# The rows of maxima of 27 heads put by ScalarE's DMA queue instead of SyncE's

## The chip, the cores and the metric

The kernel runs on one core of a Trainium2 chip. Times are device microseconds of one execution. The engines are TensorE (PE, with its weight loads as PEld), VectorE (DVE), ScalarE (ACT), GpSimd (POOL) and SyncE (SP). SP computes nothing here: it issues DMAs, one after the other. ACT computes, and can issue DMAs too; an instruction of an engine's queue starts after the ones ahead of it.

## The reference: bucketed attention and a feed-forward block

```python
q_bucket = np.sum(q_bits * powers, axis=-1)      # bits: sign of q @ proj, 6 of them
mask = q_bucket[:, :, :, None] == k_bucket[:, :, None, :]
scores = np.where(mask, scale * np.matmul(q, k.transpose(0, 1, 3, 2)), -1000000000.0)
attn = np.exp(scores - np.max(scores, axis=-1, keepdims=True))
attn = attn / (np.sum(attn, axis=-1, keepdims=True) + 1e-09)
attn_out = np.matmul(attn, v)                    # 4 batches, 8 heads, 768 tokens, 64 wide
# then, over 3072 tokens of width 512:
h = x @ w_in                                     # 512 -> 2048
g = np.where(h >= 1, h, np.where(h <= -1, 0.0, (h + 1) ** 2 / 4))
out = g @ w_out                                  # 2048 -> 512
```

All in float32, from which the kernel's matmuls work with pairs of a high and a low part.

## The kernel before

Attention comes first (to about 441 us), then the feed-forward block. Attention is one list of units: 32 heads (`hd`), in each two halves of 384 queries, in each six blocks of 128 keys, so 12 units per head, `g` from 0 to 383. A unit (`s_unit`, L432) multiplies keys by queries in two matmuls into one PSUM tile `s` (L439 and L440), ACT takes the exponential twice, as a rounded `ph` (L448) and in full (L453), and `lo_unit` subtracts the two to `pl`, on POOL where `pool_lo(g)` says so and on VectorE otherwise (L39, a helper). Four units later `pv_unit` multiplies both with V (L473, L475, L477).

The mask and the row maxima enter S as extra rows of the operand tiles `T1` and `T2`: rows 0 to 7 of `T2[...][:, 0, h]` hold bits of the query's bucket and, in row 7, the negated maximum of each query. That maximum is found one to two heads ahead: PE multiplies once more (`max_mm`, L361, into the single PSUM pair `smax`), VectorE reduces (`nm`, L378), POOL clamps, PE transposes (L416), ACT copies the result to a small tile `te` (L421), and two DMAs leave from `te`: one sets row 7 of `T2` (L423), the other stores flags to DRAM (L425). The first L440 of the head reads row 7 and so waits for the first of these DMAs. `max_put` of a head runs behind the sixth unit of the head before, so six units lie between it and that matmul. Two buffers of `te` take turns.

Each engine runs its instructions in the order in which this list writes them. So on SP, the row's DMA stands behind whatever the units before wrote there: the finished output of the head before (`xd`, L487, and `sd`, L488), staged weights (L108), loads of the next pair's q and k (`raw`, L174), moves between operand tiles (L190), bits (L316). On ACT, what follows the copy to `te` is the sign of the bits (`neg`, L243), the exponentials, in the even heads (head 4 on) the cast of the next pair's V (L323), and the copies of outputs (L483).

In the kernel before, the row's DMA is issued by ACT for heads 3 and 4 and by SP for heads 5 to 31 (heads 0 and 1 set theirs in another way, and head 2 in halves).

Of the kernel before, what the change touches and what calls it, by code (L numbers as in the profile page):

```python
# [11 lines left out]
F32 = mybir.dt.float32  # L12
# [107 lines left out]
NQK, NV, NP_ = 3, 2, 7  # L120
# [9 lines left out]
def attention(ctx, tc, wst, T1, T2, qk, v, pj, cv, x_d, s_d, e_d, tasks, shared):  # L130
    nc = tc.nc
# [286 lines left out]
    def max_put(hd):  # L418
        pr, h = hd // 2, hd % 2
        te = small.tile([2 * NJ, P], F32R, name="te")  # L420
        (nc.vector.tensor_copy if hd == 0 else nc.scalar.copy)(out=te, in_=mx.pop(hd)[0:2 * NJ, 0:P])  # L421
        if pr > 0:
            (nc.sync if hd > 4 else nc.scalar).dma_start(out=T2[pr % NQK][7:8, 0, h, :].bitcast(F32),  # L423
                                                         in_=te[0:NJ, :].bitcast(F32))
        nc.sync.dma_start(out=e_d[hd // H][hd % H:hd % H + 1, :], in_=te[NJ:2 * NJ, :].bitcast(F32))  # L425

# [199 lines left out]
    at(12, move, 1, 2)  # L626
    at(12, max_tr, 0, 0)
    at(12, max_put, 0)
    at(10, load_raw, 2)
    at(13, move, 1, 3)  # L630
# [5 lines left out]
    for t in VB[1:]:  # L636
        at(12, lambda t=t: nc.gpsimd.memset(t[:, :, 1].bitcast(F32), 0.0))
    at(17, max_tr, 1, 1)
    at(17, max_put, 1)
    at(19, half_put, 2, 0, 1)  # L640
    at(24, half_put, 2, 1)
    for h, g in enumerate((20, 2 * NU + 1)):
        at(g, lambda h=h: nc.gpsimd.memset(T2[0][32:33, 0, h].bitcast(F32), 0.0))
    for hd in range(NH):
        pr, h = hd // 2, hd % 2
        g = hd * NU
        if 0 < hd < NH - 2:
            gc, gt = ((30, 32), (41, 43))[hd - 1] if hd < 3 else (g + NU + SHIFT - 1, g + NU + SHIFT + 1)
            at(gc, max_clamp, hd + 2, nc.gpsimd)
            at(gt, max_tr, hd + 2)  # L650
            at(gt, max_put, hd + 2)
# [730 lines left out]
```

## Time and profile before

| | |
|---|---|
| median of 3 runs | 928.15 us (926.03 to 929.7) |
| the profiled execution | 927.39 us, span 925.6 us |
| PE busy | 904.9 us, 98% of the span |
| ACT busy, whole span | 667.1 us, 72% |
| ACT busy, 80 to 427 us (attention with rows put by SP) | 315.65 of 347 us |
| PE idle at L440, ended by `t<-te` | 3.4 us, 6 times |
| PEld idle at L440, ended by `t<-te` | 6.1 us, 9 times |

A row of the timeline has the start in us, the length in us, the engine, the line and the operation, and in square brackets how long the engine was idle before it and what ended that. SPq and ACTq are instructions of the queues that issue DMAs; they do not count as the engine's busy time. A matmul of 384 columns is shown 0.33 us long, but the next one may start 0.16 us after it.

### The profile page before, as it was taken

The page shows a single profiled execution, that of the slowest core. Times are in us where ns is not written, and L with a number is a line of the kernel's source. Part 1 is how long each engine was busy: PE and PEld are TensorE (multiplying, and loading weights), DVE is VectorE, ACT ScalarE, POOL GpSimd, SP SyncE. Part 2 cuts the span into 40 slices and gives each one's busy share as a digit, 9 for nine tenths or more (in the row PEclk, how much of TensorE's full clock was granted, in tenths as well). Part 3 has the DMA queues.
Part 4 walks back from the last instruction along what each step waited for, and adds up shares of the span by engine and source line. Part 5 has one row for each costly group of instructions (what it writes and reads, how often), then busy time and mean ns, then how long its engine had stood idle before and what let it go on. Part 6 is the DMA issues. An engine that isn't in the chain of part 4 may idle for free.

```text
span 925.6 us, 15771 instructions
## 1 busy us (share of the span) xinstructions
PE 904.9 (98%) x5050; PEld 846.4 (91%) x5050; DVE 746.3 (81%) x1319; ACT 667.1 (72%) x1471; POOL 352.3 (38%) x464
## 2 busy tenths in 40 slices
PE   8999999999999999999999999999999999999997
PEld 7789999999998999999999998989999999999996
DVE  8988889888897889887798888878877788765564
ACT  7889998999988999999656566555565555554454
POOL 7877777888787787778100000000000000000000
PEclk9999999999999999999999999999999999999999
DMA  5774676666666676564496388987559564464431
GB/s 159 195 201 109 181 195 194 191 181 180 175 179 187 188 193 184 140 185 123 144 307 228 114 245 299 317 259 204 149 152 271 156 200 127 147 178 126 125 91 68
DMA packets 95689, 167.66 MB, mean 181 GB/s; under 512 B 14532, under 2 KB 52536, under 8 KB 95608
## 3 DMA queue, kind: packets, MB, share of 16 engines
q1 hardware_dynamic: 95344, 166.63, 62.3%
q8 instruction: 40, 0.66, 0.3%
q14 instruction: 41, 0.34, 0.1%
q10 hardware_dynamic: 264, 0.03, 0.0%
HBM read 106.13 MB, written 33.96 MB: 151 GB/s over the span
## 4 chain that ended last, share of the span: by engine, by line
PE 71%; DVE 11%; ACT 7%; DMA 5%; issue 4%; POOL 1%; DVEq 0%; ACTq 0%; SPq 0%; POOLq 0%
PE y L913 24%; PE h L1145 16%; PE h L1050 6%; DMA t<-te 4%; PE s L440 4%; PE smax L361 4%; PE o L477 3%; PE o L473 3%; PE o L475 3%; PE s L439 3%; DVE nm L378 3%; DVE pl L39 3%; PE o L237 2%; ACT ph L448 2%; ACT s L453 1%
## 5 line engine op out<-in xcount | busy, mean ns | idle before, releaser
L448 ACT ACTIVATE ph<-s 128x384 fp32r<-128x384 f32 x380 | 193.0, 508 | 31.3 <-PE s L440 28.5
L39 POOL TENSOR_TENSOR pl<-pf,ph 128x384 fp32r<-128x384 f32 x154 | 156.0, 1019 | 67.9 <-ACT pf L453 67.7
L378 DVE TENSOR_REDUCE nm<-smax 128x1 f32<-128x768 f32 x168 | 160.1, 953 | 22.5 <-PE smax L361 19.4
L39 DVE TENSOR_TENSOR pl<-s,ph 128x384 fp32r<-128x384 f32 x230 | 123.6, 549 | 22.6 <-ACT s L453 18.3
L878 DVE SCALAR_TENSOR_TENSOR t<-t 128x384 f32<-128x384 f32 x128 | 71.3, 557 | 85.9 <-ACT z L873 85.6
L440 PE MATMUL s<-t 128*128 128x384 f32 x384 | 126.2, 329 | 3.5 <-DMA t<-te 3.4
L477 PE MATMUL o<-pl,va 128*128 128x384 f32 x384 | 125.7, 327 | 1.0 <-POOL pl L39 0.6
L473 PE MATMUL o<-ph,va 128*128 128x392 f32 (+1 forms) x384 | 126.0, 328 | 0.6 <-DVE neg L248 0.6
L475 PE MATMUL o<-ph,vb 128*128 128x392 f32 (+1 forms) x384 | 125.8, 328 | 0.0
L439 PE MATMUL s<-t 128*128 128x384 f32 x384 | 125.7, 327 | 0.0
L913 PE MATMUL y<-t,ghi 128*128 128x512 f32 x384 | 118.3, 379 | 0.7 <-DMA wc<-tmp 0.7
L453 ACT ACTIVATE s<-s 128x384 f32<-128x384 f32 x226 | 115.7, 512 | 0.0
L361 PE MATMUL smax<-t 128*128 128x384 f32 x336 | 85.9, 337 | 4.0 <-DVE nm L378 3.3
L883 ACT CAST ghi<-z 128x384 fp32r<-128x384 f32 x129 | 64.9, 503 | 32.0 <-DVE z L879 31.7
L873 ACT ACTIVATE z<-t,m 128x384 f32<-128x384 f32 x128 | 78.8, 615 | 4.2
L440 PEld LDWEIGHTS s<-t 128*128 128x128 f32 x384 | 72.5, 189 | 6.3 <-DMA t<-te 6.1
L913 PEld LDWEIGHTS y<-t,ghi 128*128 128x128 f32 x384 | 71.0, 189 | 7.4 <-ACT ghi L883 1.3
L453 ACT ACTIVATE pf<-s 128x384 f32<-128x384 f32 x154 | 77.5, 503 | 0.0
L1145 PE MATMUL h<-wbig,t 128*128 128x384 f32 x399 | 76.6, 326 | 0.3 <-DVE wsq L1164 0.3
L879 DVE TENSOR_TENSOR z<-t,z 128x384 f32<-128x384 f32 x128 | 71.4, 558 | 4.5
L477 PEld LDWEIGHTS o<-pl,va 128*128 128x128 f32 x384 | 72.6, 189 | 2.4 <-POOL pl L39 1.5
L913 PE MATMUL y<-woh,glo 128*128 128x512 f32 x192 | 73.1, 381 | 0.8 <-DVE glo L887 0.8
(208 smaller groups left out, 2003.3 us busy)
## 6 DMA issues: line engine op xcount, KB each, us to landing
t<-wc SPq DMA_DIRECT2D x92, 256.0 KB
t<-t SPq DMA_DIRECT2D x60, 384.0 KB
wraw<-wc SPq DMA_DIRECT2D x76, 256.0 KB
raw<-in_qk_dram SPq DMA_DIRECT2D x14, 768.0 KB
wraw<-in_w_in_dram SPq DMA_DIRECT2D x16, 512.0 KB
wraw<-in_w_out_dram SPq DMA_DIRECT2D x16, 512.0 KB
t<-ed SPq DMA_DIRECT2D x36, 192.0 KB
xd<-xs SPq DMA_DIRECT2D x32, 192.5 KB
```

Of the source, the lines that this page charges most:

```text
L39: eng.tensor_tensor(out=out, in0=a, in1=b, op=ALU.subtract)
L361: nc.tensor.matmul(out=into(ps[:, 0:HS]), lhsT=t2[:, 0, h, i * P:(i + 1) * P], rhs=streamed(t2[:, 1, h, hf * HS:(hf + 1) * HS]), start=Tru ...
L378: nc.vector.tensor_reduce(out=nmp(hd)[:, i:i + 1], in_=smax[hd][:, :, 0:HS], axis=AX.XY, op=ALU.max, negate=True)
L439: nc.tensor.matmul(out=into(ps[:, 0:HS]), lhsT=t1[:, 1, h, ks], rhs=streamed(t1[:, 0, h, sl]), start=True, stop=False)
L440: nc.tensor.matmul(out=into(ps[:, 0:HS]), lhsT=t2[:, 1, h, ks], rhs=streamed(t2[:, 0, h, sl]), start=False, stop=True)
L448: nc.scalar.activation(out=ph[:, 0:HS], in_=ps[:, 0:HS], func=AF.Exp, scale=SCALE)
L453: nc.scalar.activation(out=pf, in_=ps[:, 0:HS], func=AF.Exp, scale=SCALE)
L473: nc.tensor.matmul(out=into(o[:, 0:w]), lhsT=wa, rhs=streamed(ph[:, 0:w]), start=(jj == 0), stop=False)
L475: nc.tensor.matmul(out=into(o[:, 0:w]), lhsT=wb, rhs=streamed(ph[:, 0:w]), start=False, stop=False)
L477: nc.tensor.matmul(out=into(o[:, 0:HS]), lhsT=wa, rhs=streamed(pl), start=False, stop=(jj == NJ - 1))
L913: nc.tensor.matmul(out=into(ys[c][m]), lhsT=g_[:, m * P:(m + 1) * P], rhs=streamed(w), start=(first and k == 0), stop=(last and k == 2))
L1145: nc.tensor.matmul(out=into(ps), lhsT=w[:, cs], rhs=streamed(x), start=(n == 0 and s not in (2, 3, 6)), stop=(n == 5), skip_group_check=True)
```

## The change

One expression: the engine that issues the DMA of row 7. What is copied, from where and to where, is the same.

```diff
         if pr > 0:
-            (nc.sync if hd > 4 else nc.scalar).dma_start(out=T2[pr % NQK][7:8, 0, h, :].bitcast(F32),
+            nc.scalar.dma_start(out=T2[pr % NQK][7:8, 0, h, :].bitcast(F32),
                                                          in_=te[0:NJ, :].bitcast(F32))
         nc.sync.dma_start(out=e_d[hd // H][hd % H:hd % H + 1, :], in_=te[NJ:2 * NJ, :].bitcast(F32))
```

On ACT, at the place in head 8 (an even head) where the row of head 9 is put; `va` is the cast of V, `neg` the sign of the bits. Before:

```order
L421 CAST te<-s 12x128
L243 ACTIVATE neg<-o_142 32x384
L448 ACTIVATE ph_163<-s 128x384
L453 ACTIVATE pf<-s 128x384
L323 CAST va_156<-vraw 128x6x2x64
L448 ACTIVATE ph_164<-s 128x384
L453 ACTIVATE s<-s 128x384
```

And now, as far as it differs:

```order
L421 CAST te<-s 12x128
L423 DMA t_1_82<-te 1x6x128
L243 ACTIVATE neg<-o_142 32x384
L448 ACTIVATE ph_163<-s 128x384
L453 ACTIVATE pf<-s 128x384
```

The DMA stands directly behind the copy that feeds it, and ahead of `neg`; the rest of ACT's order is the same.

On SP, the place in an odd head where the row of the next even head (head 8, whose operand tile is `t_1_82`) was put; `wq` is a staged weight, `em` the store of the flags:

```order
 L488 DMA sd_63<-xs 1x768
 L108 DMA wq_98<-wsq 128x512
-L423 DMA t_1_82<-te 1x6x128
 L425 DMA em_72<-te 6x128
 L190 DMA t_2_80<-t_2_83 64x1536
```

SP no longer issues the row; the output, the weight and the flags keep their places. The same happens at each of the 27 heads. The orders on PE, VectorE and POOL do not change.

## The prediction

> **What bounds the kernel now.** I read the page first, then the waits of the attention stretch, then single stretches of the timeline. The page:
>
> ```profile
> PE 904.9 (98%) x5050; PEld 846.4 (91%) x5050; DVE 746.3 (81%) x1319; ACT 667.1 (72%) x1471; POOL 352.3 (38%) x464
> PE y L913 24%; PE h L1145 16%; PE h L1050 6%; DMA t<-te 4%; PE s L440 4%; PE smax L361 4%; PE o L477 3%; PE o L473 3%; PE o L475 3%; PE s L439 3%; DVE nm L378 3%; DVE pl L39 3%; PE o L237 2%; ACT ph L448 2%; ACT s L453 1%
> ```
>
> PE bounds the kernel as a whole, but the page's averages mix two stages, and the change lies in attention only. The 4% for `t<-te` in the chain (37 us) is not what the transfer costs: the chain follows it from issue to landing, while PE works on other things for most of that time. The stretch where the rows move, and the same stretch's waits, say more (columns of the first row: length, then busy us and count of PE, PEld, DVE, ACT, POOL; of the others: us in total, times, longest):
>
> ```profile
> 80.00:427.00 347.00, 338.79 (x2014) 324.16 (x2014) 302.56 (x454) 315.65 (x773) 275.18 (x348) 1.00 0.64 177
> ACT ph L448 <- PE s L440: 24.2, 61, 0.7
> DVE pl L39 <- ACT s L453: 14.4, 22, 1.0
> PEld smax L361 <- DVE nm L378: 10.7, 25, 0.6
> PEld s L440 <- DMA t<-te: 6.1, 9, 1.2
> PE s L440 <- DMA t<-te: 3.4, 6, 0.9
> ```
>
> ACT is busy 315.65 of 347 us (91%) here, not 72%, and 24.2 of its 31 idle us are waits for PE: a cover, but a broken one. PE's largest wait is for VectorE's maxima (`nm`); the rows of maxima come second. VectorE itself waits for ACT's exponentials 22 times, so an ACT delay can reach PE by way of VectorE.
>
> **What the change moves.** 27 issues, heads 5 to 31, go from SP's queue to ACT's; heads 3 and 4 are there already and give the price:
>
> ```profile
> L423 SPq DMA_DIRECT2D t<-te x27: 755/765/785, 81.8 to 425.3; - x27
> 57.45 0.25 ACT L421 CAST te<-s 12x128 fp32r<-12x128 f32 x1
> 57.73 0.73 ACTq L423 DMA_DIRECT2D t<-te  x1
> 58.51 0.48 ACT L243 ACTIVATE neg<-o 32x384 f32<-32x384 f32 x1 [0.81 <-PE o L477]
> 70.50 0.68 ACTq L423 DMA_DIRECT2D t<-te  x1
> 71.22 0.49 ACT L448 ACTIVATE ph<-s 128x384 fp32r<-128x384 f32 x1 [0.75 <-PE o L477]
> 73.99 0.33 PE L439 MATMUL s<-t 128*128 128x384 f32 x1
> 74.15 0.33 PE L440 MATMUL s<-t 128*128 128x384 f32 x1
> ```
>
> The label blames PE, but the idle time is exactly the issue: ACT does nothing for 0.81 and 0.75 us while its queue issues. So 27 puts put 27 x 0.78 = 21 us on ACT. On the whole stretch that nearly fits into the 31 idle us; the question is where.
>
> The Trainium skill (DMA: Bandwidth & Descriptors, section "Issuing engines are not separate DMA queues") holds that issuing from another engine saves only the issue time on the sequencer, which it calls usually small. By its 50 ns for sequencer dispatch (same page, "Anatomy of one DMA — SWDGE (gpsimd) path") I estimate 27 x 0.05 = 1.4 us on ACT and the change would be a small gain; the rows above show fourteen times that, and they decide.
>
> **The gain.** A put on SP is late and lands late (the chain's rows are start, us; a wait's length stands in square brackets):
>
> ```profile
> 200.25 0.25 ACT L421 CAST te<-s 12x128 fp32r<-12x128 f32 x1
> 199.20 1.91 SPq L487 DMA_DIRECT2D xd<-xs  x1
> 202.13 0.76 SPq L423 DMA_DIRECT2D t<-te  x1
> 202.13 4.83 DMA t<-te
> 206.36 0.33 PE L439 MATMUL s<-t 128*128 128x384 f32 x1
> 207.00 0.43 PE L440 MATMUL s<-t 128*128 128x384 f32 x1 [0.31 <-DMA t<-te]
> ```
>
> The row of head 14 is ready at 200.50, SP issues it 1.63 us later because xd and what follows it stand ahead, and it lands 4.83 us after issue. PE's two S matmuls start 0.64 us apart where 0.16 is normal (73.99 and 74.15 above): 0.48 lost. PE's idle of 3.4 us hides 0.17 at each of its 6 places (0.33 long at a pace of 0.16), so about 4.4, and with the three short ones that only the weight load shows some 4.9 us are lost in all. On ACT's queue the issue comes right behind the copy, and row 4 was there by 74.15, at most 3.65 us after its issue. A row issued at 200.53 would then land by 204.2, 2.3 us ahead of need. I take all nine stalls as gone. What is late next is VectorE's maximum:
>
> ```profile
> 208.44 0.95 DVE L378 TENSOR_REDUCE nm<-smax 128x1 f32<-128x768 f32 x1
> 209.73 0.49 PE L361 MATMUL smax<-t 128*128 128x384 f32 x2
> 182.04 0.96 DVE L378 TENSOR_REDUCE nm<-smax 128x1 f32<-128x768 f32 x1 [0.20 <-PE smax L361]
> 183.48 0.49 PE L361 MATMUL smax<-t 128*128 128x384 f32 x2
> ```
>
> At head 14 VectorE works without idle into the reduction that ends at 209.39; PE's next maximum at 209.73 needs it and can come 0.3 earlier, not 0.48. At head 12 (0.91 lost, the label says 0.75 idle) the reduction can start 0.2 earlier, which lets the maximum at 183.48 come 0.6 earlier. So some 60% of 4.9 is kept, 2.9 us; from this goes what ACT's own delay has left on VectorE there (next part).
>
> **The cost.** Two kinds of places. First the even heads, where the rows of the odd heads 5 to 27 are put (12 puts):
>
> ```profile
> 187.08 0.25 ACT L421 CAST te<-s 12x128 fp32r<-12x128 f32 x1
> 187.59 0.48 ACT L243 ACTIVATE neg<-o 32x384 f32<-32x384 f32 x1 [0.26 <-PE o L237]
> 188.85 0.83 ACT L323 CAST va<-vraw 128x768 fp32r<-128x768 f32 x1
> 189.96 0.50 ACT L453 ACTIVATE s<-s 128x384 f32<-128x384 f32 x1
> 197.50 0.49 ACT L448 ACTIVATE ph<-s 128x384 fp32r<-128x384 f32 x1 [0.69 <-PE s L440]
> 190.55 0.56 DVE L39 TENSOR_TENSOR pl<-s,ph 128x384 fp32r<-128x384 f32 x1 [0.86 <-ACT s L453]
> 191.02 0.95 DVE L378 TENSOR_REDUCE nm<-smax 128x1 f32<-128x768 f32 x1
> 192.11 0.34 PE L361 MATMUL smax<-t 128*128 128x384 f32 x1
> 196.49 0.59 PE L361 MATMUL smax<-t 128*128 128x384 f32 x2 [0.22 <-DVE nm L378]
> ```
>
> The put goes between 187.33 and 187.59; 0.81 of idle replaces 0.26, so `neg` and all behind it slide 0.55 us. ACT has no further idle time until 197.50: the cast of V (0.83) stands behind it. The exponential that ends at 190.46 ends at 191.01, and VectorE, which already waits 0.86 us for it, starts its subtraction 0.55 later. The reduction behind it ends at 192.52 instead of 191.97, and PE's maximum matmul at 192.11 must wait for it, some 0.45 us; at 196.49, where PE waits for VectorE already, the full 0.55 has arrived. PE has no slack to win it back: its matmuls follow each other at 0.16 us. So 12 x 0.55 = 6.6 us. At heads 5 and 7 there is no 0.26 to use (the next row), so 0.79 each: together 7.1 us.
>
> ```profile
> 81.84 0.48 ACT L243 ACTIVATE neg<-o 32x384 f32<-32x384 f32 x1
> 204.11 0.49 ACT L448 ACTIVATE ph<-s 128x384 fp32r<-128x384 f32 x1 [0.20 <-PE s L440]
> 208.67 0.49 ACT L448 ACTIVATE ph<-s 128x384 fp32r<-128x384 f32 x1 [0.33 <-PE s L440]
> ```
>
> Second, the odd heads, where the rows of 6 to 28 are put (12 puts; 200.25 is one). No cast of V follows, ACT's slide of about 0.6 is cut by waits for PE at 204.11 (0.20) and 208.67 (0.33), and VectorE does not wait for ACT at a point where PE waits for VectorE. I cost these at nothing, hidden under those waits, except that about 0.3 is still on VectorE around 207 and eats the gain there: of 2.9 us I keep 1.5. Without that cover they would cost as the first kind, another 12 x 0.55 = 6.6.
>
> Third, rows 29 to 31, put where no `neg` follows:
>
> ```profile
> 424.40 0.25 ACT L421 CAST te<-s 12x128 fp32r<-12x128 f32 x1 [0.27 <-PE s L416]
> 424.83 0.49 ACT L448 ACTIVATE ph<-s 128x384 fp32r<-128x384 f32 x1 [0.18 <-PE s L440]
> ```
>
> Head 31's comes 15 us before the end of attention, with ACT at work almost throughout: 0.81 less 0.18 is a slide of 0.6. PE uses an exponential four units later, so between 0 and 0.6 shows; I take 0.5 for all three. SP loses 27 x 0.765 = 21 us of issues; PE waits for no transfer of SP's but these rows there, so I price that at nothing (bounds 0 to 1 us gain).
>
> Sum: 7.1 + 0.5 - 1.5 = +6.1 us. The profiled execution took 927.39 us, 0.76 under the median of the three runs (928.15). 927.39 + 6.1 = 933.5, which I forecast; it would be 934.3 on the median.
>
> **Rivals.** (1) The cover holds on even heads too: place, the maximum at 192.11; if that slide costs PE a third (0.2 us of 0.55, because VectorE catches up in the 0.5 us it idles later in the head), the cost is 2.5 + 0.5, and the gain kept is between 2.9 and 4.9: 927.4 + 3 - 3.9 = 926.5, not slower. It decides from a slide under about 0.25 us per head. For it: the 24.2 us that ACT waits for PE. Against it: none of them lies between 187.6 and 197.5. (2) The issue is dearer on ACT while SP issues its large loads: SP's own xd took 1.91 us at 199.20 behind a load, against 0.77 for SP's puts. If ACT's put is held the same way at the 12 odd heads (1.1 more each, of which the waits of 0.20 and 0.33 hide 0.5), that is 12 x 0.6 = 7 more: 940.5. Against it: 0.73 and 0.68 are steady, if only twice seen. (3) The move does not do what it says: the rows still queue behind SP's traffic and land as late as now, the stalls stay and the delay is paid, 927.4 + 7.6 = 935. Here the skill's rule that all issuers share the same 16 DMA engines and interleave would speak for it; row 4's 3.65 us against 4.83 for head 14's bears that out only weakly. (4) Both effects are hidden, 927 to 928.5.
>
> **How the numbers follow.** Forecast 0.58, its own range 930 to 937; rival 1 0.15, 2 0.14, 3 0.08, 4 0.05. A change of under 0.5% (4.6 us) cannot be told from none by a measurement of this kernel, so slower means above 932.8. From the forecast 0.36 lies above and 0.22 below; rivals 2 and 3 are slower (0.22); rival 1 gives 0.05 faster and 0.10 the same; rival 4 the same. Slower 0.58, same 0.37, faster 0.05. The low end is 927.4 + 3.5 (half of the even heads' cost) - 3.9 = 927; the high end reaches to rival 2: 940.
>
> **What would show it.** The waits for `t<-te` at L440 vanish (else rival 3). ACT's queue shows 29 puts of about 0.7 us, each with some 0.8 us idle behind (over 1.2 in odd heads: rival 2). At the copy behind each V cast, VectorE's wait for ACT grows from 0.86 to 1.4, and PE's waits for `nm` grow from 10.7 us to about 17; if they stay, rival 1 is right. FFN, 445 us on, keeps its length. The forecast is wrong if attention ends earlier than before.

## The result: slower, 934.91 us

The changed kernel took 934.91 us (median of 6 runs, 933.43 to 935.61), the kernel before 927.43 us on the same chip; the ratio is 1.0077, 95% interval 1.0063 to 1.0091. The forecast was 933.5 us, range 927 to 940. The page of the profile after, whose execution took 934.82 us:

```profile
span 933.0 us, 15779 instructions
PE 909.0 (97%) x5050; PEld 844.9 (91%) x5050; DVE 743.4 (80%) x1319; ACT 663.9 (71%) x1471; POOL 352.0 (38%) x464
```

The first and last matmul `y` of the feed-forward block, of the kernel before and then of the changed one (the last two times of a row are the first and the last start):

```profile
L913 PE MATMUL y<-t,ghi x384: 379/379/483, 449.4 to 866.6; 128*128 128x512 f32 x192
```

```profile
L913 PE MATMUL y<-t,ghi x384: 379/379/483, 456.9 to 874.6; 128*128 128x512 f32 x192
```

The block starts 7.5 us later and keeps its length (417.2 and 417.7 us). All of the loss is in attention. The waits of the changed kernel from 80 to 427 us:

```profile
PEld smax L361 <- DVE nm L378: 20.5, 42, 1.4
DVE neg L248 <- ACT neg L243: 17.9, 21, 1.3
PE smax L361 <- DVE nm L378: 7.4, 27, 1.1
PEld s L440 <- DMA t<-te: 2.6, 6, 0.7
PE s L440 <- DMA t<-te: 1.0, 3, 0.5
```

PE's waits for VectorE's maxima about doubled (the weight load's from 10.7 us, the matmul's from 2.9). Its waits for the row fell by more than half (6.1 and 3.4 before), but did not vanish.

To compare kernels I use one count throughout: from the first L440 of head 4 to that of head 31, for each matmul of PE, the time since the start of the one before, less its normal pace (164 ns for 384 columns), where that is over 40 ns, added up by the line of the matmul that came late. It is worked out from the timeline's rows, for one profiled execution of each kernel, so a single wait that falls differently shows in it. "Even" and "odd" are the lengths of heads 4 to 28 and of heads 5 to 27, from first L440 to first L440.

| | even | odd | head 29 | head 30 | late at L361 | at L440 | at L477 |
|---|---|---|---|---|---|---|---|
| before | 167.2 | 163.8 | 13.03 | 11.31 | 11.3 | 5.0 | 1.5 |
| after | 176.2 | 161.1 | 13.89 | 11.90 | 21.6 | 2.0 | 2.4 |
| e1, odd heads' rows on ACT | 174.7 | 164.8 | 13.45 | 11.88 | 18.6 | 6.1 | 2.9 |
| e2, even heads' rows on ACT | 169.0 | 161.6 | 13.81 | 11.31 | 14.3 | 1.7 | 2.4 |
| e3, before, cast later | 164.4 | 165.6 | 13.04 | 11.30 | 7.5 | 8.5 | 1.0 |
| e4, after, cast later | 168.8 | 167.5 | 13.89 | 11.90 | 19.8 | 2.9 | 3.1 |
| e5, e1 and cast later | 167.2 | 169.3 | 14.47 | 11.88 | 9.4 | 10.8 | 5.0 |
| e9, rows on POOL | 164.9 | 163.1 | 15.00 | 12.02 | 10.1 | 6.2 | 1.8 |
| e10, even heads' rows on POOL | 165.4 | 164.9 | 14.85 | 11.31 | 10.4 | 8.0 | 1.0 |
| e11, before, raw load later | 180.1 | 158.7 | 13.03 | 11.31 | 14.7 | 0.3 | 6.2 |
| e12, before, raw load in halves | 169.0 | 158.9 | 13.03 | 11.31 | 15.2 | 0.2 | 1.0 |

So of +7.8 us after, the even heads lost 9.1, heads 29 and 30 lost 1.45, and the odd heads won 2.7. A head's row is put in the head before it: the row of head 29 in head 28, which is counted with the even heads, those of 30 and 31 in heads 29 and 30.

The place of the prediction's timeline, head 12, in the changed kernel. First ACT, then VectorE, then PE's maxima:

```profile
189.07 0.25 ACT L421 CAST te<-s 12x128 fp32r<-12x128 f32 x1
189.35 0.69 ACTq L423 DMA_DIRECT2D t<-te  x1
190.09 0.48 ACT L243 ACTIVATE neg<-o 32x384 f32<-32x384 f32 x1 [0.76 <-PE s L440]
191.35 0.83 ACT L323 CAST va<-vraw 128x768 fp32r<-128x768 f32 x1
...
190.60 0.55 DVE L248 TENSOR_TENSOR neg<-o,neg 32x384 f32<-32x384 f32 x1 [0.82 <-ACT neg L243]
193.05 0.56 DVE L39 TENSOR_TENSOR pl<-s,ph 128x384 fp32r<-128x384 f32 x1 [1.04 <-POOL pl L39]
193.52 0.95 DVE L378 TENSOR_REDUCE nm<-smax 128x1 f32<-128x768 f32 x1
...
194.52 0.59 PE L361 MATMUL smax<-t 128*128 128x384 f32 x2 [0.23 <-DVE nm L378]
198.99 0.59 PE L361 MATMUL smax<-t 128*128 128x384 f32 x2 [0.22 <-DVE nm L378]
```

ACT's idle time before `neg` is 0.76 us instead of 0.26. VectorE waits 0.82 for `neg` and 1.04 for the exponential behind the cast (the label names POOL, whose subtraction had ended at 192.56; the exponential ends at 192.95, and VectorE starts at 193.05). PE now waits for `nm` once more, at 194.52, still within head 12; the wait at 198.99, in head 13, is the one that stood at 196.49 before. The chain that ended last goes through the put itself (ACTq L423 at 189.35).

### The profile page after: what moved, and what is told of

The parts are those of the page before. It is cut to its first block, busy times and chain, and to the rows that moved or that the text cites. A ratio compares the mean times of both kernels' runs of the same rounds, so it can differ in the third digit from the quotient of the medians.

```text
span 933.0 us, 15779 instructions
## 1 busy us (share of the span) xinstructions
PE 909.0 (97%) x5050; PEld 844.9 (91%) x5050; DVE 743.4 (80%) x1319; ACT 663.9 (71%) x1471; POOL 352.0 (38%) x464
## 4 chain that ended last, share of the span: by engine, by line
PE 63%; DVE 13%; ACT 10%; DMA 5%; issue 5%; POOL 2%; ACTq 1%; DVEq 0%; SPq 0%; POOLq 0%
PE y L913 24%; PE h L1145 16%; PE h L1050 6%; ACT ph L448 4%; DVE nm L378 3%; PE smax L361 3%; DVE pl L39 3%; PE s L440 3%; PE s L439 2%; PE o L477 2%; PE o L473 2%; PE o L475 2%; DMA t<-te 2%; POOL pl L39 2%; ACT pf L453 1%
## 5 line engine op out<-in xcount | busy, mean ns | idle before, releaser
L39 DVE TENSOR_TENSOR pl<-s,ph 128x384 fp32r<-128x384 f32 x230 | 123.6, 549 | 26.2 <-POOL pl L39 12.2
L477 PE MATMUL o<-pl,va 128*128 128x384 f32 x384 | 125.8, 328 | 1.7 <-POOL pl L39 0.9
L440 PE MATMUL s<-t 128*128 128x384 f32 x384 | 125.8, 328 | 1.0 <-DMA t<-te 1.0
L361 PE MATMUL smax<-t 128*128 128x384 f32 x336 | 88.6, 345 | 8.8 <-DVE nm L378 7.8
L361 PEld LDWEIGHTS smax<-t 128*128 128x128 f32 x336 | 54.6, 188 | 24.8 <-DVE nm L378 21.4
L477 PEld LDWEIGHTS o<-pl,va 128*128 128x128 f32 x384 | 72.6, 189 | 3.4 <-POOL pl L39 1.8
L440 PEld LDWEIGHTS s<-t 128*128 128x128 f32 x384 | 72.6, 189 | 2.6 <-DMA t<-te 2.6
## 6 DMA issues: line engine op xcount, KB each, us to landing
xd<-xs SPq DMA_DIRECT2D x32, 192.5 KB
```

The lines of the kernel that those rows point to most:

```text
L39: eng.tensor_tensor(out=out, in0=a, in1=b, op=ALU.subtract)
L361: nc.tensor.matmul(out=into(ps[:, 0:HS]), lhsT=t2[:, 0, h, i * P:(i + 1) * P], rhs=streamed(t2[:, 1, h, hf * HS:(hf + 1) * HS]), start=Tru ...
L440: nc.tensor.matmul(out=into(ps[:, 0:HS]), lhsT=t2[:, 1, h, ks], rhs=streamed(t2[:, 0, h, sl]), start=False, stop=True)
L477: nc.tensor.matmul(out=into(o[:, 0:HS]), lhsT=wa, rhs=streamed(pl), start=False, stop=(jj == NJ - 1))
```

## Which of the puts cost: e1 and e2

e1 puts the odd heads' rows on ACT and leaves the even heads' with SP; e2 does the reverse. Against the kernel before:

```diff
# e1
-            (nc.sync if hd > 4 else nc.scalar).dma_start(
+            (nc.scalar if hd <= 4 or hd % 2 else nc.sync).dma_start(
# e2
+            (nc.scalar if hd <= 4 or hd % 2 == 0 else nc.sync).dma_start(
```

> Only the rows of the odd heads (5 to 31, 14 puts, all but the last two made in even heads) go to ACT's queue; the even rows stay with SP. Theory (ACT's slide reaches PE through VectorE in the even heads, and nowhere else before the last heads): the even heads 4 to 28 grow by 0.5 to 0.8 us each as in the changed kernel, 9 us in all, the stalls at L440 stay (4.9 us lost), so 8 to 10 us over the kernel before, 935.5 to 937.5: dearer than the whole change. Rival (each put costs the same wherever it stands, 7.5 / 27 = 0.28 us): 14 x 0.28 = 3.9, 931.3.

e1: 936.91 us, ratio 1.0092 (1.0073 to 1.0111), as the theory had it.

> Only the rows of the even heads (6 to 30, 13 puts, made in odd heads) go to ACT's queue. Theory: no cost in the even heads beyond 0.1 us, the stalls at L440 shrink from 4.9 to under 2 us, head 30's put costs up to 0.6: 1.5 to 2.5 us under the kernel before, 925 to 926. With the odd rows' run the two differences add up to the change's 7.5. Rival (each put 0.28): 13 x 0.28 = 3.6 more, 931.

e2: 928.58 us, ratio 0.9999 (0.9986 to 1.0012). Neither expectation held. The waits of e1 and then of e2, 80 to 427 us, with two rows of e2's timeline:

```profile
PEld smax L361 <- DVE nm L378: 17.8, 37, 0.7
PEld s L440 <- DMA t<-te: 7.2, 9, 1.2
PE smax L361 <- DVE nm L378: 6.6, 27, 0.4
```

```profile
PEld smax L361 <- DVE nm L378: 13.5, 29, 1.4
PEld s L440 <- DMA t<-te: 2.3, 6, 0.6
...
183.38 0.50 POOL L179 CAST t<-raw 128x384 fp32r<-128x384 f32 x1 [2.59 <-DMA raw<-in_qk_dram]
186.93 0.43 PE L477 MATMUL o<-pl,va 128*128 128x384 f32 x1 [1.19 <-POOL pl L39]
```

e1 carries the whole cost: with its puts alone the even heads grow 7.5 us. e2 has most of the gain at L440 (5.0 to 1.7 us late), wins 2.1 in the odd heads, and loses 0.8 in head 29, where the row of head 30 is put. The 1.8 us that its even heads lose, where it puts nothing, are one wait: head 12 alone grew 2.07, because POOL waited 2.59 us for raw data and PE then for POOL (the two rows; 1.35 us late at L477 and 0.50 at L416); the other twelve even heads are 0.28 shorter together. In the kernel before, such a wait of 2.81 us for raw data stands in head 20.

Of the 3.3 us that the odd heads of e2 win at L440, 1.2 come back at L361 in the same heads, behind the copy to `te`. There L361 is 1.8 us late in the odd heads before, and also in e12 below, where the rows are on time too but SP puts them; it is 3.0 late in e2 and 2.0 in the changed kernel. So the twelve puts in odd heads cost PE 1.2 us in e2 and 0.2 in the changed kernel.

## Does the cast behind the put make it dear: e3, e4, e5

The cast of V is moved nine units on, into the odd head: alone (e3), with the change (e4), and with e1's put (e5).

```diff
-            at(gv, cast_v, pr + 1, nc.scalar)
+            at(gv + (9 if pr > 1 else 0), cast_v, pr + 1, nc.scalar)
```

> The kernel before, with the cast of V moved nine units on (from the unit behind the row's put in each even head from 4 on to the fourth unit of the odd head); rows by SP as before. Theory: VectorE's wait of 0.86 us for ACT behind the cast goes, and with it PE's waits of 0.53 at the maximum in the odd heads 5 to 27: 3 to 6 us under the kernel before, 921 to 924. Rival (VectorE's own weight steps make those waits): no change within 1 us, or up to 3 us slower because the cast now delays the odd heads.

> The same move of the cast of V, in the changed kernel (27 rows by ACT). Theory (the put is exposed because the cast of V stands behind it and ACT has no idle time for 10 us): without the cast, ACT's waits for PE come back in the even heads and hide the put; this kernel stands at most 3 us above the one with the cast moved and rows by SP. Rival (the put's delay reaches PE whatever stands behind it): the distance between the two stays at 6 to 8 us.

> Only the odd heads' rows by ACT (14 puts, made in even heads and before the last two heads), with the cast of V moved out of the even heads. Theory (the cast of V behind the put is what leaves ACT without cover): in the run with all rows by ACT and the cast moved, the even heads from 8 on cost only 0.27 us each over the cast-moved kernel with rows by SP; so 12 x 0.3 to 0.4 and 1.4 for the last rows: 4 to 6 us over that kernel's 926.9, 931 to 933, against 936.9 with the cast in place. Rival (the put costs as much without the cast): 8 to 9.5 over it, 935 to 936.5.

| | median, us | ratio, interval | against e3 |
|---|---|---|---|
| e3 | 926.93 | 0.9985 (0.9973 to 0.9998) | |
| e4 | 932.67 | 1.0046 (1.0029 to 1.0063) | +5.7 |
| e5 | 935.42 | 1.0081 (1.0067 to 1.0095) | +8.5 |

e3's waits, then e5's:

```profile
PEld s L440 <- DMA t<-te: 9.5, 11, 1.8
PEld smax L361 <- DVE nm L378: 7.5, 19, 0.6
PEld o L477 <- POOL pl L39: 0.6, 1, 0.6
```

```profile
PEld s L440 <- DMA t<-te: 12.1, 11, 1.7
PEld smax L361 <- DVE nm L378: 7.7, 17, 0.7
PEld o L477 <- POOL pl L39: 5.5, 12, 2.1
```

The theory lost in all three, in an instructive way; the rival's numbers held in e3 and e5, and e4 fell between the two. e3 took 2.8 us out of the even heads, and the rows came 3.5 us later relative to PE: hardly a gain. e5's puts cost the even heads 2.8 us over e3 instead of 7.5, so the cast behind the put does carry the slide to L361. But the time came out elsewhere: at L477, where PE waits for POOL's subtraction, and at L440, where SP issued the even heads' rows on average 1.16 us behind their copy instead of 0.79, with the copy no later ahead of the matmul (5.61 and 5.52 us). Of the 4.0 us more at L477, 2.0 stand in heads 29 and 30, where POOL also waited 2.70 us for a staged weight (0.86 in e3), so how much of that part the puts cost is open. ACT is busy 91% of the stretch in the kernel before, and what it stands still surfaced in part at whichever wait was next (5.7 us over e3 in e4, which has the early rows too, 8.5 in e5): moving the neighbour decided where more than whether.

## Is it the issue on ACT, or the earlier transfer: e9 and e10

POOL is idle for an exponential of ACT just where the row is put. e9 lets it issue all 27 rows, e10 only the even heads' (13 rows); odd rows stay with SP in e10.

```diff
# e9
-            (nc.sync if hd > 4 else nc.scalar).dma_start(
+            (nc.gpsimd if hd > 4 else nc.scalar).dma_start(
# e10
+            (nc.scalar if hd <= 4 else nc.sync if hd % 2 else nc.gpsimd).dma_start(
```

> The 27 rows are issued by GpSimd (POOL) instead of ScalarE (ACT): as early as in the changed kernel, but on an engine that in the kernel before is busy 275 of 347 us of this stretch and mostly idle 1.0 to 1.75 us for ACT's exponential right where the row is put. Theory (the whole cost of the change is the 0.78 us that ACT stands still per put; an issue on an engine with idle time at that place is free): the cost is gone, 927 us, between 925.5 and 928.5, and the row stalls at L440 stay near the 1.8 us of the changed kernel, since the transfers share the same DMA engines. Rival (the cost comes with the earlier transfer itself, from whichever engine): 933 to 935.5 again. Second rival (an issue holds POOL for over 2 us, so its subtractions come late and PE waits for them at L477): over 936.

> Only the rows of even heads 6 to 30 (14 in all with none of the odd ones) are issued by POOL; those of odd heads stay with SP, which is on time there. Theory: 925 to 927.5, no more than 2.5 us better than before, because the even rows still need 5 to 6 us to land behind the moves. Rival (the earlier transfer costs): 928.5 to 931.

e9: 929.73 us, ratio 1.0012 (0.9999 to 1.0025). e10: 928.73 us, ratio 1.0004 (0.9989 to 1.0018). The waits of e9, one of its puts, three rows of its chain of waits (start, length), and a row of VectorE in head 29:

```profile
POOL t L423 <- ACT te L421: 22.7, 26, 1.2
POOL pl L39 <- ACT pf L453: 15.5, 32, 1.5
PEld smax L361 <- DVE nm L378: 9.8, 16, 2.6
PEld s L440 <- DMA t<-te: 7.5, 11, 2.0
...
200.36 0.61 POOL L423 DMA_DIRECT2D t<-te  x1 [1.19 <-ACT te L421]
...
174.13 6.14 DMA t<-te
200.36 5.95 DMA t<-te
226.42 5.92 DMA t<-te
...
412.34 3.15 DVE L790 SCALAR_TENSOR_TENSOR raw<-t,xsv,raw 128x384 f32<-128x384 f32 x1
```

This separates the two causes. The rows leave nearly as early as in the changed kernel (0.29 us after the copy ends at 200.07, a length of 0.25 after 199.82 in ACT's row; 0.03 there), POOL needs 0.61 us per issue, and PE's waits for `nm` are back at 9.8 us. Of the ratio of 1.0077, 1.0012 is left: the loss was the issue on ACT, not the earlier transfer. The issue is not free on POOL either, but POOL waits less for ACT in return (15.5 us for `pf` and 22.7 for `te`, instead of 56.5 for `pf`). The time missed its range by 1.2 us, on a chip where the kernel before took 928.87. Head 29 takes 2.0 us longer in e9 and 1.8 in e10: there a VectorE instruction between two reductions (L790, the last row above) takes 3.15 and 2.79 us instead of 1.17, and PE's maximum waits 2.28 and 1.82 us for the reduction behind it. Why it is slow when POOL puts the row was not tested.

And neither gains: an even head's row still needs 5 to 6 us from issue to the matmul, from whichever queue. The stalls at L440 are 6.2 us late in e9, not near 1.8 as expected. e10 is 8.0 us late at L440 and loses the 1.8 us in head 29; its expected gain did not come for these two reasons. Its time lies in the rival's range, but e9 speaks against the rival's cause.

## Why the even heads' rows are late: e6, e7, e8, e11, e12

In the changed kernel the row of head 14 stands in the chain of waits as

```profile
202.98 6.57 DMA t<-te
209.59 0.43 PE s L440
```

issued 1.6 us sooner after its copy than before, and still too late by 0.5 us. By the trace's records of single DMA packets, the rows of odd heads 13 to 27 have landed 1.4 to 1.8 us after ACT issues them; those of even heads 12 to 26 begin to move 3.8 to 4.4 us after it and have landed after 5.4 to 6.1. From the issue to the first packet, the DMA engines are busy 0.24 of the time at head 13's row and 0.95 at head 14's (columns as in the prediction's stretch from 80 to 427 us; the last two are the DMA engines' busy share and GB/s):

```profile
189.35:190.77 1.42, 1.42 (x10) 1.42 (x9) 0.60 (x2) 0.66 (x2) 0.00 (x0) 1.00 0.24 60
202.98:207.38 4.40, 4.40 (x29) 4.34 (x28) 3.33 (x7) 3.65 (x9) 2.28 (x4) 1.00 0.95 223
```

What differs is what SP has issued just ahead: three moves of 384 KB and the load of raw q and k, 768 KB. e6 (before), e7 (after) and e8 (e6 with e3's cast) set the three moves behind the row; e11 sets the raw load there instead.

```diff
# e6, e7, e8: moves 0 to 2 of the pair
-                at(g0 + (3 + (pr == 1) if pr < 2 else 13), move, pr + 2, n)
-            at(g0 + (6 if pr < 2 else 14), move, pr + 2, 2)
+                at(g0 + (3 + (pr == 1) if pr < 2 else 18), move, pr + 2, n)
+            at(g0 + (6 if pr < 2 else 18), move, pr + 2, 2)
# e11
-                at(g0 + (7 if pr < 2 else 14), load_raw, pr + 3)
+                at(g0 + (7 if pr < 2 else 18), load_raw, pr + 3)
```

> The kernel before, with the three moves between operand tiles (3 x 384 KB) that SP issues ahead of each even head's row issued behind it instead; rows by SP. Theory (an even row is late because the DMA engines are still at work on 1.9 MB of moves and loads, whichever queue it is on): SP is held less at the output's DMA, the row lands within 3 us of its issue, the stalls at L440 (4.9 us lost) go, and 1.5 to 2.5 us of it stay as gain: 925 to 926. Rival (the row is late for SP's order alone): the issue is earlier by under 0.5 us, landing still 5 us, stalls stay within 1 us, no change.

> The same move in the changed kernel. Theory: the even rows land within 3 us of ACT's issue instead of 5 to 6, the remaining 1.8 us lost at L440 go, the ACT cost stays: 0.5 to 1.5 us under the changed kernel, 933.4 to 934.4. Rival (ACT's queue is slow for another reason): the stalls stay, no change.

> The kernel before with both: the cast of V later and the moves behind the row; rows by SP. The cast-moved kernel loses 8.2 us at L440 to late rows; without these, and with VectorE's wait behind the cast gone, 3 to 6 us less than that kernel: 921 to 924. Rival (what the row no longer holds up, VectorE's maxima do): within 1.5 us of it, 925.5 to 927.

> The kernel before, with the load of raw q and k for pr+3 (about 0.77 MB) four units later, behind the row, the moves where they were. If that load is what holds the even rows, by queueing ahead of them on SP and on the DMA engines, the L440 stalls fall from 4.9 us to under 2 and the time to 924.5 to 926.5. Rival (the moves alone hold the rows): stalls 4 to 5 us, time within 1 us of the kernel before.

| | median, us | ratio, interval |
|---|---|---|
| e6 | 966.31 | 1.0415 (1.04 to 1.0431) |
| e7 | 953.1 | 1.0275 (1.0256 to 1.0293) |
| e8 | 980.84 | 1.057 (1.0551 to 1.0589) |
| e11 | 934.62 | 1.0068 (1.0052 to 1.0084) |

All four times missed their theory, and in all four the row was on time. e7's waits, then e11's:

```profile
PEld smax L361 <- issue: 14.8, 9, 2.3
PE smax L361 <- DMA t<-bits: 14.3, 12, 2.0
```

```profile
POOL t L179 <- DMA raw<-in_qk_dram: 20.2, 10, 3.7
PEld o L477 <- POOL pl L39: 6.6, 8, 2.1
PEld s L416 <- POOL nmr L407: 5.9, 10, 0.6
```

In e6, e7 and e8 it is the moves, and the bits that SP issues behind them, that now come late (the first bits at 217.43 in e7 at head 14, at 207.17 in the changed kernel): the next pair's maxima (L361) read both, the label names the bits, which landed last, and PE's weight load waits up to 2.3 us at a time in e7 and 3.5 in e8 (even heads' sum 194.4 us in e7, 210.2 in e6, 167.2 before). The expectations had left out this reader of the moved tiles. In e11 nothing waits for the row (e11's L440 is 0.3 us late in all), but POOL's cast waits 20.2 us for raw data instead of 4.1, and its subtractions and clamps come late at L477 and L416. Either way the row needs less ahead of it. An estimate from the trace of before says roughly how much: three moves (1152 KB), the raw load (768 KB) and `xd` (192.5 KB) are 2.16 MB; at 177 GB/s, the mean from 80 to 427 us, they take 12.2 us, and from 194.83, where the first is issued, that ends at 207.0, where the row landed (202.13 + 4.83). That the two agree so well is partly chance: in these 12.2 us the engines moved 233 GB/s, so other transfers were among them. Half of the raw load less would by the same estimate end 2.2 us sooner.

So e12, on the kernel before: the raw load in two halves, the first where it was, the second behind the row. The first is read at unit 24, the second from unit 31 on.

```diff
-    def load_raw(pr):
-        raws[pr] = work.tile([P, 2, S], F32, name="raw", bufs=1)
-        for sl in (slice(0, HS), slice(HS, S)) if pr == 1 else (slice(0, S),):
+    def load_raw(pr, hfs=None):
+        if hfs != (1,):
+            raws[pr] = work.tile([P, 2, S], F32, name="raw", bufs=1)
+        for sl in [slice(hf * HS, (hf + 1) * HS) for hf in hfs] if hfs else \
+                (slice(0, HS), slice(HS, S)) if pr == 1 else (slice(0, S),):
...
-                at(g0 + (7 if pr < 2 else 14), load_raw, pr + 3)
+                if pr < 2:
+                    at(g0 + 7, load_raw, pr + 3)
+                else:
+                    at(g0 + 14, load_raw, pr + 3, (0,))
+                    at(g0 + 18, load_raw, pr + 3, (1,))
```

> The kernel before (rows by SP), with the load of raw q and k for pr+3 in two halves (0.39 MB each, 384 of the 768 tokens): the first where the whole load was (two units ahead of the even row), the second four units later, right behind the row. Each half is first read by POOL 10 units and more behind its new place. Theory (the even rows are late because of what is loaded just ahead of them, and e11 lost only because POOL then waited for the whole load): the stalls at L440 fall from 4.9 us to under 1.5, POOL's wait for raw (L179) stays under 7 us (20.2 in e11, 4.1 before), and the time falls by 2 to 4 us, ratio 0.9957 to 0.998. Rival (half a load ahead is enough to hold the row): stalls 3 to 5 us, ratio 0.9985 to 1.0005. Second rival (POOL waits for the late half all the same): ratio 1.002 to 1.006.

923.97 us against 928.57 on the same chip, ratio 0.9954 (0.9938 to 0.9969): faster than both kernels. Its timeline at head 14's row (lines are two further down than in the others: L425 is the row's put, L442 the second S matmul, L363 the maximum), then its waits:

```profile
197.52 1.24 SPq L176 DMA_DIRECT2D raw<-in_qk_dram  x1
201.75 0.77 SPq L425 DMA_DIRECT2D t<-te  x1
203.07 0.63 SPq L176 DMA_DIRECT2D raw<-in_qk_dram  x1
205.85 0.33 PE L441 MATMUL s<-t 128*128 128x384 f32 x1
206.01 0.33 PE L442 MATMUL s<-t 128*128 128x384 f32 x1
...
PEld smax L363 <- DVE nm L380: 14.4, 32, 0.6
PE smax L363 <- DVE nm L380: 2.9, 13, 0.3
```

The two S matmuls follow each other at 0.16 us: the row, still issued by SP and no earlier behind its copy than before, is there within 4.26 us. No wait for it is left, and none of POOL for raw data. The odd heads win 4.9 us, the even heads give 1.9 back at the maxima. In the profiled executions that is 3.0 us; over the runs the medians differ by 4.6, a little more than the 2 to 4 us expected.

## Why the prediction was right, and where it was not

- **The price of a put** was right: ACT's 29 puts take 677 to 733 ns, each with 0.75 to 0.81 us of standing still behind it, in odd heads as in even ones. Rival 2 (dearer behind SP's loads) fell with that. Neither ACT's issue nor POOL's (0.61 us) comes near the 0.05 us that the prediction set against it; 21 us are fifteen times its 1.4, not fourteen.

```profile
L423 ACTq DMA_DIRECT2D t<-te x29: 677/683/733, 57.4 to 431.6; - x29
203.70 0.48 ACT L243 ACTIVATE neg<-o 32x384 f32<-32x384 f32 x1 [0.75 <-PE s L440]
```

- **Even heads, 7.1 us**: 6.7 in e1 for the twelve rows of heads 5 to 27, put in heads 4 to 26 (its 7.5 hold head 28 with the row of head 29 too). The way through `neg`, the exponential, VectorE's reduction and L361 is the one the trace shows; e5 adds that the cast behind it decides the place more than the amount (8.5 us in all over e3, against 9.3 for e1 over the kernel before). Rival 1 (cover) fell.
- **The gain, 1.5 us net**: the size held, the reason did not. The odd heads won 2.7, and heads 4 to 26 grew 8.3, which is 1.6 beyond e1's 6.7, so 1.1 net. The step "a row issued at 200.53 would then land by 204.2, I take all nine stalls as gone" failed: the late L440 went from 5.0 to 2.0 us, since the row takes 6.57 us, not 3.65. The price came from a row of head 4, during whose transfer the DMA engines were hardly busy (0.22 from 70.50 to 72.20 us). "Some 60% is kept" was borne out where the stalls really went: e12 wins 4.9 in odd heads and keeps 3.0.
- **Odd heads' puts at nothing**: nearly so in the changed kernel, 0.2 us late at L361 behind the copy, but 1.2 in e2 and none in e12. So part of VectorE's slide can reach PE there.
- **Rows 29 to 31, 0.5 us**: 2.2 (head 28 grew 0.78, head 29 0.86, head 30 0.59). Here nearly the whole slide of 0.6 to 0.8 shows for each, not one in all. This is the term that was mis-sized most, and it makes the difference between +6.1 and +7.8: 6.7 - 1.1 + 2.2 = 7.8. That the gain's size came out near 1.5 is luck, since its reason failed (above).
- **Rival 3** (the rows land as late, the delay is paid) named 935, nearer than the forecast; its mechanism was half true. The rows of even heads do stand behind SP's loads on whichever queue, but more than half of the stalls went, and the cost was larger than it assumed. The Trainium skill (DMA: Bandwidth & Descriptors, "Issuing engines are not separate DMA queues") has the DMAs of all issuing engines run on the same 16 DMA engines. The traces agree: 6.57 us for head 14's row on ACT, 5.92 to 6.14 for such rows on POOL. The same section calls the time to issue "usually small relative to the DMA itself". Here it was 0.75 to 0.81 us against 5.4 to 6.1 in even heads and 1.4 to 1.8 in odd ones, on the engine that had no time to spare. Rival 4 (both hidden) fell.
- Of the signs named, VectorE's wait at the copy behind the cast came out at 1.04 us under another label, not at 1.4; the other part is the 0.82 for `neg`. PE's waits for `nm` reached 20.5 us, not 17.

Still open: whether e2, without the one wait in its head 12, would have gained, and how e12 would do together with e3's cast or POOL's put, which was not run.

## What to carry to other kernels

Before moving a DMA's issue to a compute engine for an earlier start, price the issue as engine time (here 0.78 us each) and look at what that engine has to spare at that place; an engine that waits there anyway took it almost for nothing here (e9). Then ask whether the transfer is late because it is issued late, or because of the bytes issued ahead of it on the shared DMA engines: here no other queue made the kernel faster, and splitting one large load so that its second half stands behind the small urgent transfer did. And expect a stall that is taken away to come back in part at the next wait of the same engine; in e12 40% did.

## What the runs showed of the hardware that was not expected

A transfer of 3 KB on a queue of its own can be held for about 4 us by large transfers issued ahead on another queue: 5.4 to 6.1 us to landing in even heads, 1.4 to 1.8 in odd ones, with the same engine, queue and size. The Trainium skill (DMA: Bandwidth & Descriptors, "Queues, rings and completion order") has each DMA engine turn between the queues that have work for it, packet by packet. By itself that would let a row of 12 packets through soon; in these traces its first packet moved only 3.8 to 4.4 us after the issue. What holds it was not settled. And in e6 and e8, PE's granted clock from 75 to 427 us fell to 0.97 and 0.95, against 1.00 before and in e7, where PE waits for the bits as well; from 460 to 900 us it was 1.00 in all four. Why was not tested. A row of e8's stretches, with the clock as the third number from the end:

```profile
75.00:427.00 352.00, 318.62 (x1781) 303.54 (x1780) 271.59 (x407) 280.62 (x685) 243.99 (x311) 0.95 0.57 156
```
